# The first layer's weights summed by identity products on TensorE, and one network piece moved ahead of the state products

## The chip, the cores and the metric

The kernel runs on one core of one Trainium2 chip. The metric is the device time of one execution in microseconds (us), lower is better. The engines are named as in the profile: PE is TensorE (PEld its weight loads), DVE is VectorE, ACT is ScalarE, POOL is GpSimd, SP is SyncE, which here only issues transfers.

## The reference

A recurrent attention (batch 4, heads 8, sequence 768, head size 48) is followed by a two-layer network with a PReLU between the layers. The attention's output, laid out as 3072 tokens of 384, is the network's input.

```python
f = sigmoid(f_logit)
for t in range(S):
    state = f[:, :, t, :, None] * state + einsum('bhd,bhe->bhde', k[:, :, t], v[:, :, t])
    y[:, :, t] = einsum('bhd,bhde->bhe', q[:, :, t], state)
x = y.transpose(0, 2, 1, 3).reshape(3072, 384)
h = x @ w_in                                   # 384 x 2048
g = maximum(h, 0) + alpha * minimum(h, 0)
out = g @ w_out                                # 2048 x 384
```

The weights w_in and w_out arrive as 64-bit numbers; the kernel rebuilds them in float32 on the chip.

## The kernel before, in words

**Steps.** The work is cut into 12 steps (lines 725 to 757): 6 chunks of 128 tokens, and in each chunk two pairs of batches. A step handles 2 x 128 = 256 tokens. While step n's attention runs, the network works on step n-1 and the preparation on step n+1.

**Pieces.** Each stage is a Python generator, and each `yield` ends a piece:
- `prepare` (L261; P for the own step, Q for the coming one): loads f, q, k, v; sigmoid and copies on ACT (L282 to L285), then products of decays on DVE (qd L290, kr L293, fs L297), the us copies on ACT (L317), the scans ps and ss (L320, L322), us L324, k L350, the products kh, ks, us, q (L333, L371, L377, L390), and in the last pieces ks L401, us L407, q L409 and the A copies on ACT (L422).
- `carry` (O): first piece the off products (L447, in the first chunk L457 too) with ACT's ad and A copies (L461, L465) and, in the first chunk, the transposes pk (L474) with the ksn copies (L477). Second piece the state products pd (L487) and the update of vs (L497, L501, in the first chunk ACT's copy L503).
- `attend` (S): for each of two batches raw (L523) with the DVE's masked copies (L529) and qu (L538) with its own (L544, in the first chunk L560); then A copies on ACT (L566); then py (L577); then y (L586) on ACT and the transposition to xT, which in step 0 is made on PE (xt L595, ACT copies L597) and later by transfers.
- `network` (n): eight pieces of 6 products ph (L620) with ACT's neg (L625) and two DVE gates (L627), every fourth followed by the sums S (L701); then the second layer, in step 0 plainly (po L640), later with seven half-size products in place of eight (pa to pe, L659).
- `halves_of_w_out` (W, L703): sums of w_out's quarters on DVE (L720) for those seven products.

**The weights.** `load_weights` (L168) makes the pieces of both weights, 8 of 128 x 768 columns each. `upper` (a for w_in, b for w_out) issues a raw transfer on SP (L197; RAWS = 4 buffers) and takes the positive and the negative high parts on ACT, pos (L202) and neg (L204), TOPS = 3 buffers each. `rests` (w for w_in, v for w_out) does lead n (L210, LEADS = 4 buffers), rest n-1 (L223), power n (L216, POWERS = 1) and both n-1, all on DVE but for the last. lead is the high part of a weight in bf16, rest is the low part, put into the weight's place in float32, and `both` adds the high part to it: for w_in's pieces on DVE (L228, since AT_ONCE = 8 takes them all), for w_out's by an accumulating transfer from POOL (L230).

**Order.** PE, DVE and ACT run in exactly the order in which the program issues their instructions (a manual schedule, L745). That order is written by hand: a string for each of the first four steps (`first`, L726 to L731) and one for all others (`usual`, L732). A letter is a piece of the generator with that letter, a number behind it the count of pieces. Transfers are issued by SP and POOL, each in program order.

**PSUM.** Two pools: `pair` has 2 buffers of two banks (off, pk, pd, raw, qu, py), `bank` has 4 buffers of one bank (idle, xt, ph, po, pa to pe). A buffer is given in turn, so an instruction that takes one waits for the readers of the one before.

Of the kernel before, what the change touches and what calls it, by code (L numbers as in the profile page):

```python
# [11 lines left out]
BF16 = mybir.dt.bfloat16  # L12
# [3 lines left out]
ALU = mybir.AluOpType  # L16
# [7 lines left out]
NC2 = C // CH  # L24
NB = DB // 4
WP = 768
AT_ONCE = 8
IDLE = 40
RAWS, TOPS, POWERS, LEADS = 4, 3, 1, 4

# [2 lines left out]
def kernel(  # L33
# [30 lines left out]
    nc = tc.nc  # L64
    B, NC, _, HP, _ = qT.shape
# [7 lines left out]
    W = U * HP * C  # L73
# [15 lines left out]
    const = ctx.enter_context(tc.tile_pool(name="const", bufs=1))  # L89
# [9 lines left out]
    def bank(name):  # L99
        return psn.tile([128, 512], F32, tag="net", name=name)  # L100

    om = const.tile([128, NF], F32, tag="om", name="om")
    w_in_sb = const.tile([128, NK, DF], F32, tag="w_in", name="w_in_sb")
# [31 lines left out]
    for m in range(1, NB):  # L135
        lo = UO[m] + (4 if m == 1 else 0)
        n = NB - m
# [4 lines left out]
    for half in range(2):  # L142
        for m in range(1, NQ):
            n = NQ - m
            lo = 16 * half + 4 if m == 1 else VO[m] + 4 * n * half
# [11 lines left out]
        nc.gpsimd.memset(vs[bp], 0.0)  # L157
    ident = const.tile([128, 128], F32, tag="ident", name="ident")
    make_identity(nc, ident)
    nc.gpsimd.tensor_scalar(om, om, -1.0, 1.0, ALU.mult, ALU.add)  # L160


# [5 lines left out]
    def load_weights(dst, src, name):  # L168

        rows_ = NK if dst is w_in_sb else 1  # L180
        pieces_ = dst.shape[1] * dst.shape[2] // WP
        if rows_ == 1:
            dst = dst.rearrange("p a n -> p (a n)").unsqueeze(1)
        width = WP // rows_
        words = src.rearrange("p (a n) -> p a n", a=rows_).bitcast(I16)
        at_once = AT_ONCE if rows_ > 1 else 0
        got = {}

        def of(n):
            return dst[:, :, n * width:(n + 1) * width]  # L190

        def by_row(t):
            return t.rearrange("p (a n) -> p a n", a=rows_)

        def upper(n):
            raw = stage.tile([128, WP, 4], I16, tag="raw", name=f"{name}_raw{n}", bufs=RAWS)
            nc.sync.dma_start(out=raw.rearrange("p (a n) four -> p a (n four)", a=rows_)[:, :, 0:4 * width - 1],  # L197
                              in_=words[:, :, 4 * n * width + 1:4 * (n + 1) * width])

            top = raw[:, :, 2]  # L200
            pos = stage.tile([128, WP], I16, tag="pos", name=f"{name}_pos{n}", bufs=TOPS)
            nc.scalar.activation(pos, top, AF.Relu, bias=bias[:, 0:1], scale=8.0)  # L202
            neg = stage.tile([128, WP], I16, tag="wneg", name=f"{name}_neg{n}", bufs=TOPS)
            nc.scalar.activation(neg, top.bitcast(U16), AF.Relu, bias=bias[:, 1:2], scale=8.0)  # L204
            got[n] = raw, pos, neg

        def lead(n):
            raw, pos, neg = got[n]
            t = stage.tile([128, WP], BF16, tag="lead", name=f"{name}_lead{n}", bufs=LEADS)
            nc.vector.tensor_tensor(t, pos.bitcast(BF16), neg.bitcast(BF16), ALU.subtract)  # L210
            got[n] = raw, t

        def power(n):
            raw, t = got[n]
            p = stage.tile([128, WP], BF16, tag="power", name=f"{name}_power{n}", bufs=POWERS)
            nc.vector.tensor_scalar(p.bitcast(I16), t.bitcast(I16), -128, None, ALU.bitwise_and)  # L216
            got[n] = raw, t, p

        def rest(n):
            raw, t, p = got.pop(n)  # L220
            got[n] = t
            low = raw.bitcast(U32)[:, :, 0]
            nc.vector.scalar_tensor_tensor(of(n), by_row(low), 2.0 ** -36, by_row(p), ALU.mult, ALU.mult)  # L223

        def both(n):
            t = by_row(got.pop(n))
            if n < at_once:
                nc.vector.tensor_tensor(of(n), of(n), t, ALU.add)  # L228
            else:
                nc.gpsimd.dma_start(out=of(n), in_=t, accum_op=ALU.add)  # L230

        def uppers():
            for n in range(pieces_):
                upper(n)
                yield

        def rests():
            for n in range(pieces_ + 1):
                if n < pieces_:
                    lead(n)  # L240
                if n:
                    rest(n - 1)
                if n < pieces_:
                    power(n)
                if n:
                    both(n - 1)
                yield

        return uppers(), rests()

    def rows(par):
        return slice(64 * par, 64 * par + D)
# [450 lines left out]
    def halves_of_w_out():  # L703
# [12 lines left out]
        for to, x_, y_, op in ((t3, b22, b12, ALU.subtract), (t2, t3, b11, ALU.add), (t4, t2, b21, ALU.subtract),  # L716
                               (b12, b12, b11, ALU.subtract)):
            for h in range(2):
# [5 lines left out]

    steps = [(bp, c) for c in range(NC) for bp in range(B // U)]
    first = (  # L726
# [4 lines left out]
    )  # L731
    usual = "S n2 S n2 O2 n Q n2 Q n2 Q S3 n Q S n Q n Q n"  # L732
    pieces = {key: part for keys, parts in (("aw", load_weights(w_in_sb, w_in, "w_in")),
                                            ("bv", load_weights(w_out_sb, w_out, "w_out")))
              for key, part in zip(keys, parts)}

# [76 lines left out]
```

## Time and profile before

| | |
|---|---|
| median of 3 runs | 633.37 us (632.31 to 634.52) |
| the profiled execution | 634.88 us, of which the span is 633.1 us and 1.8 us lie around it |
| PE busy | 593.9 us, 94% of the span, 8188 instructions |
| PE weight loads busy | 529.2 us, 84% |
| DVE busy | 512.0 us, 81%, 1035 instructions |
| ACT busy | 249.8 us, 39%, 466 instructions |
| POOL busy | 58.8 us, 9%, 107 instructions |
| costliest groups | PE ph L620 258.4 us; PE pa L659 62.0 us and pc L659 61.7 us; DVE gate L627 82.1 us |
| moved by DMA | 53.57 MB; 66% of the 16 engines' time in the first 61.8 us |

How to read it: times are in us from the start of the span, unless marked ns. A timeline line gives start, duration, engine, line of the code, operation, output<-input, the shape and "x" the count of records joined in it; in brackets is the idle time of the engine just before and what released it. A float32 product is two records. A group line ("busy, mean ns of one | idle before, releaser") sums all instructions of one line and form. Matmuls are pipelined, and a few of their records can be missing. "issue" is time in which an engine waited for nothing that the profile shows. The chain of waits is followed back from the last instruction to what released each.

### The profile page before, as it was taken

Reading aid. Unit: us, or ns where it says so; the run is one execution under the profiler, and the core shown is the slowest. Engines: PE = TensorE matmul, PEld = TensorE weight load, DVE = VectorE, ACT = ScalarE, POOL = GpSimd, SP = SyncE. Lnnn points to the kernel's source line nnn. Section 1 sums busy time; section 2 is a strip of 40 time slices with the busy share of each in tenths; the row PEclk is TensorE's granted clock in tenths of the full one; section 3 lists DMA queues with packets and bytes.
Section 4 is the critical chain, followed back from the end, with each engine's and each line's share of the span. In section 5 each row is a group of like instructions: output and inputs, shape, how many; then the busy total and the mean of one; then the engine's idle time right before and its main releaser. Section 6 shows DMA issues by size and latency. Waiting matters only on the chain.

```text
span 633.1 us, 19007 instructions
## 1 busy us (share of the span) xinstructions
PE 593.9 (94%) x8188; PEld 529.2 (84%) x8188; DVE 512.0 (81%) x1035; ACT 249.8 (39%) x466; POOL 58.8 (9%) x107
## 2 busy tenths in 40 slices
PE   2357999989999999999999999999999999999997
PEld 2356865879789889889889889889889889889997
DVE  5799999999799788888888888888888888762251
ACT  5595792541263153253253253253253253223110
POOL 9010122001001001001001001001001000000000
PEclk9999999999999999999999999999999999999999
DMA  7845796312323313313313313323323301201000
GB/s 239 279 146 182 195 295 162 58 62 73 78 54 91 79 35 85 75 46 84 72 48 84 76 45 84 68 52 84 66 54 85 61 26 26 48 7 26 26 0 26
DMA packets 70323, 53.57 MB, mean 85 GB/s; under 512 B 47296, under 2 KB 62144, under 8 KB 70240
## 3 DMA queue, kind: packets, MB, share of 16 engines
q1 hardware_dynamic: 57536, 25.37, 15.9%
q0 software_dynamic: 7312, 24.78, 13.6%
q10 hardware_dynamic: 5392, 2.21, 1.7%
q8 instruction: 65, 1.06, 0.7%
q14 instruction: 18, 0.15, 0.1%
HBM read 36.21 MB, written 4.72 MB: 65 GB/s over the span
## 4 chain that ended last, share of the span: by engine, by line
PE 73%; DVE 22%; issue 2%; ACT 1%; DMA 1%; DVEq 0%; ACTq 0%
PE ph L620 34%; PE pc L659 8%; PE pa L659 8%; PE pe L659 4%; PE pd L659 4%; PE pb L659 4%; PE qu L538 3%; PE py L577 3%; PE raw L523 3%; PE pd L487 2%; DVE gate L627 2%; DVE S L701 2%; DVE us L333 1%; DVE qd L290 1%; DVE ad L529 1%
## 5 line engine op out<-in xcount | busy, mean ns | idle before, releaser
L620 PE MATMUL ph<-xT,w_in_sb 128*128 128x256 f32 x1152 | 258.4, 383 | 0.0
L620 PEld LDWEIGHTS ph<-xT,w_in_sb 128*128 128x128 f32 x1152 | 216.7, 190 | 32.3 <-issue 2.4
L625 ACT ACTIVATE neg<-ph 128x512 f32<-128x512 f32 x96 | 57.2, 596 | 187.4 <-PE ph L620 139.6
L627 DVE SCALAR_TENSOR_TENSOR gate<-neg,om,ph 128x256 f32<-128x256 f32 x192 | 82.1, 474 | 40.7 <-ACT neg L625 40.5
L659 PE MATMUL pa<-w_out_sb,gate 128*128 128x192 f32 x352 | 62.0, 329 | 1.8 <-DVE gate L627 1.8
L659 PE MATMUL pc<-t,S 128*128 128x192 f32 x352 | 61.7, 329 | 0.0
L659 PEld LDWEIGHTS pa<-w_out_sb,gate 128*128 128x128 f32 x352 | 57.8, 190 | 3.7 <-issue 1.9
L659 PEld LDWEIGHTS pc<-t,S 128*128 128x128 f32 x352 | 57.3, 190 | 0.6
L529 DVE COPY_PREDICATED ad<-mraw,raw 128x256 f32<-128x256 int32 (+1 forms) x96 | 42.3, 441 | 7.3 <-PE raw L523 4.8
L544 DVE COPY_PREDICATED ad<-mquad,qu 128x224 f32<-128x224 int32 (+6 forms) x140 | 41.9, 299 | 6.2
L422 ACT COPY A<-q 48x512 f32<-48x512 f32 x44 | 27.2, 617 | 42.4 <-DVE q L371 38.4
L566 ACT COPY A<-ad 32x256 f32<-32x256 f32 x96 | 38.5, 401 | 1.4
L333 DVE TENSOR_TENSOR us<-us,fs 128x768 f32<-128x768 f32 (+5 forms) x60 | 36.7, 612 | 0.1
L677 ACT COPY o<-pa 128x192 f32<-128x192 f32 x11 | 3.5, 318 | 75.3 <-PE pa L659 61.5
L290 DVE TENSOR_TENSOR qd<-qd,f 128x768 f32<-128x768 f32 (+2 forms) x36 | 27.1, 753 | 6.1 <-ACT qd L285 6.1
L538 PE MATMUL qu<-us,k 48*32 48x112 f32 (+1 forms) x1536 | 27.1, 259 | 4.2 <-issue 3.0
L701 DVE TENSOR_TENSOR S<-gate 128x512 f32<-128x512 f32 x44 | 30.3, 688 | 0.8
L659 PE MATMUL pe<-w_out_sb,S 128*128 128x192 f32 x176 | 30.5, 327 | 0.3 <-ACT o L677 0.3
L659 PE MATMUL pb<-t,gate 128*128 128x192 f32 x176 | 30.4, 326 | 0.0
L659 PE MATMUL pd<-w_out_sb,S 128*128 128x192 f32 x176 | 30.4, 326 | 0.0
L577 PEld LDWEIGHTS py<-A,vs 128*64 128x64 f32 x768 | 25.7, 145 | 5.5 <-issue 2.8
L577 PE MATMUL py<-A,vs 128*64 128x64 f32 x768 | 28.1, 233 | 2.0 <-ACT vs L503 1.0
(110 smaller groups left out, 743.0 us busy)
## 6 DMA issues: line engine op xcount, KB each, us to landing
w_out_raw<-in_w_out SPq DMA_DIRECT2D x8, 767.8 KB, 5.0
w_in_raw<-in_w_in SPq DMA_DIRECT2D x8, 767.2 KB, 7.1
f<-in_fT POOLq DMA_DIRECT2D x11, 512.0 KB, 4.5
q<-in_qT POOLq DMA_DIRECT2D x11, 512.0 KB, 4.2
k<-in_kT POOLq DMA_DIRECT2D x11, 512.0 KB, 4.6
out<-o SPq DMA_DIRECT2D x24, 192.0 KB, 2.1
vs<-in_v POOLq DMA_DIRECT2D x22, 192.0 KB, 4.3
w_out_sb<-w_out_lead POOLq DMA_DIRECT2D x8, 384.0 KB, 6.3
```

Of the source, the lines that this page charges most:

```text
L290: nc.vector.tensor_tensor(qdv[d], qdv[d - 1][:, :, :, 1:5 - d], f[:, :, 1:5 - d].rearrange("p (g i) r -> p g i r", i=NB), ALU.mult)
L333: nc.vector.tensor_tensor(us[:, :, UO[m]:UO[m] + 4 * n].rearrange("p g (i r) -> p g i r", r=4), us[:, :, skip:skip + 4 * n].rearrange("p g ...
L529: nc.vector.copy_predicated(adu[:, :, :, d:4], mraw[:, d, :, d:4].bitcast(I32).unsqueeze(1).broadcast_to((128, H, NB, n)), rv[:, :, QO[d]: ...
L538: nc.tensor.matmul(qu[DB * j:DB * (j + 1), par, hp * QS + 4:hp * QS + QL], lhsT=k4[r_, g * DB:(g + 1) * DB], rhs=us[r_, g, 4:QL], start=Tr ...
L544: nc.vector.copy_predicated(ad[:, u, :, :, 4 * m:DB], mquad[:, lo:lo + n].bitcast(I32).unsqueeze(1).unsqueeze(1).broadcast_to((128, 2, HP, ...
L566: nc.scalar.copy(A[s_, u, :, s_], ad[s_, u].rearrange("p r h t -> p (r h) t"))
L577: nc.tensor.matmul(py[64 * par:64 * par + 64, u, o:o + CH], lhsT=vs[bp][:, cc, u, hd * D:hd * D + 64], rhs=A[:, u, par * HP + hp, CH * cc: ...
L620: nc.tensor.matmul(ph[:, j * T:(j + 1) * T], lhsT=w_in_sb[:, kt, m * 128:(m + 1) * 128], rhs=xT[:, kt], start=(kt == 0 and j == 0), stop=( ...
L625: nc.scalar.activation(neg, phv, AF.Relu, scale=-1.0)
L627: nc.vector.scalar_tensor_tensor(gate[:, m % NH, m // NH], neg[:, j], om[:, m:m + 1], phv[:, j], ALU.mult, ALU.add)
L659: nc.tensor.matmul(to[:, 0:DH], lhsT=of(f), rhs=by(f), start=(f == 0 and not more), stop=(f == NH - 1), skip_group_check=True)
L701: nc.vector.tensor_tensor(to, x_, y_, op)
```

## The change

Two things are changed.

1. w_in's high parts are no longer added on DVE. A new generator `sums_of_parts` (key `e`) does for each piece: into a PSUM bank the product of an identity with the float32 low part, and onto it the product of a bf16 identity (`ident16`, a new constant copied on POOL) with the bf16 high part; then ACT copies the bank back to the weight's place. A piece has 3 x 256 columns; the first bank takes 512 of them and a second 256, so a piece is two float32 and two bf16 products and two copies. The banks come from the four of `bank`. w_out's pieces are added by POOL's transfers as before. The four strings of `first` are written anew, with `e` in them: w_in's `a` and `w` come earlier, step 0's network pieces `n` and w_out's `b` and `v` are shifted.

2. In `usual`, "S n2 S n2 O2 n Q n2 Q n2 Q S3" becomes "S n2 S n O n O n Q n3 Q n Q S3"; the rest of the string is as before. On PE one ph piece goes between off (L447) and pd (L487); on DVE the scans (L320, L322) go behind the eighth gate and the sums S.

Lines of the new kernel from `summed` on are 10 higher than before (ph L620 is L630).

```diff
     make_identity(nc, ident)
+    ident16 = const.tile([128, 128], BF16, tag="ident16", name="ident16")
+    nc.gpsimd.tensor_copy(ident16, ident)
...
         def both(n):
+            nc.gpsimd.dma_start(out=of(n), in_=by_row(got.pop(n)), accum_op=ALU.add)
+
+        def summed(n):
             t = by_row(got.pop(n))
-            if n < at_once:
-                nc.vector.tensor_tensor(of(n), of(n), t, ALU.add)
-            else:
-                nc.gpsimd.dma_start(out=of(n), in_=t, accum_op=ALU.add)
+            for lo in range(0, rows_, 2):
+                rs = slice(lo, min(lo + 2, rows_))
+                at = bank(f"{name}_sum{n}_{lo}")[:, 0:width * (rs.stop - lo)].rearrange("p (a n) -> p a n", n=width)
+                nc.tensor.matmul(at, lhsT=ident, rhs=of(n)[:, rs], start=True, stop=False)
+                nc.tensor.matmul(at, lhsT=ident16, rhs=t[:, rs], start=False, stop=True)
+                nc.scalar.copy(of(n)[:, rs], at)
...
-                if n:
+                if n and rows_ == 1:
                     both(n - 1)
                 yield
 
-        return uppers(), rests()
+        def sums_of_parts():
+            for n in range(pieces_):
+                summed(n)
+                yield
+
+        return uppers(), rests(), sums_of_parts()
...
     first = (
-        "P2 a P w P a P a w O P w S a w S Q a S O a w S Q2 w S2",
-        "P a w a P w n b w n v O b v n b S v n2 P S b S v n b S v n b v n Q b n Q v b O v Q n v W Q S2 Q W n2 W Q W",
-        "O n2 S W n2 S Q S n4 O S n Q2 n Q2 S n S n Q n",
-        "S n3 S n Q n2 O Q O n2 S Q S n S Q n Q S Q n3",
+        "P a P a P a w P w P w a P a O a e w2 S2 Q S w e O S e Q2 e S2",
+        "a w n a w P2 n e2 b w n v b O v n b2 S e2 v S3 b v2 n O n b v Q b P v n3 b v Q n S Q v W n S Q n Q W3 Q",
+        "O n S W n2 S n S Q S n4 O Q n Q n S n Q S Q n2 Q",
+        "S n2 S n2 O Q n3 Q n O S n Q S2 Q S n Q n Q n2",
     )
-    usual = "S n2 S n2 O2 n Q n2 Q n2 Q S3 n Q S n Q n Q n"
-    pieces = {key: part for keys, parts in (("aw", load_weights(w_in_sb, w_in, "w_in")),
+    usual = "S n2 S n O n O n Q n3 Q n Q S3 n Q S n Q n Q n"
+    pieces = {key: part for keys, parts in (("awe", load_weights(w_in_sb, w_in, "w_in")),
                                             ("bv", load_weights(w_out_sb, w_out, "w_out")))
               for key, part in zip(keys, parts)}
```

More of the change, by code (lines that the diff above doesn't have):

```diff
@@ L26 @@
 WP = 768
-AT_ONCE = 8
 IDLE = 40
@@ L185, in load_weights @@
         words = src.rearrange("p (a n) -> p a n", a=rows_).bitcast(I16)
-        at_once = AT_ONCE if rows_ > 1 else 0
         got = {}
```

## The prediction

> **What bounds the kernel now.** I read the chain of waits first, then the busy time by stretch, then the timelines of VectorE (DVE), ScalarE (ACT) and TensorE (PE) up to 160 us, and last one usual step. The chain, over the whole span:
>
> ```profile
> PE 73%; DVE 22%; issue 2%; ACT 1%; DMA 1%; DVEq 0%; ACTq 0%
> ```
>
> In order of time it is two stories. Up to 160 us most pieces are DVE, without a break from 89.6 to 160.0 (PE stands in it at 20 to 32 and 62 to 84). After that it is PE. The busy time by stretch (length, then busy us and instructions of PE, PEld, DVE, ACT, POOL, granted clock, DMA share, GB/s) says the same:
>
> ```profile
> 0.00:61.80 61.80, 31.02 (x764) 26.57 (x765) 49.53 (x91) 38.81 (x62) 20.46 (x53) 1.00 0.66 210
> 61.80:160.60 98.80, 95.02 (x1378) 77.53 (x1378) 95.52 (x184) 50.58 (x90) 13.89 (x18) 0.98 0.52 141
> 160.60:633.10 472.50, 467.87 (x6048) 425.14 (x6048) 366.90 (x762) 160.39 (x315) 24.45 (x36) 1.00 0.23 56
> ```
>
> The reader sees: in the first stretch PE is half idle, DMA is two thirds busy and DVE is busy 80%. In the second DVE and PE are both full. In the third PE alone is full, 468 of 472 us. So up to 160 us a DVE us counts, if nothing else is late at the same moment; after that only PE time counts.
>
> The DVE part that is changed, with its neighbours:
>
> ```profile
> 22.86 0.95 DVE L228 TENSOR_TENSOR w_in_sb<-w_in_sb,w_in_lead 128x768 f32<-128x768 f32 x1
> 23.73 0.55 DVE L210 TENSOR_TENSOR w_in_lead<-w_in_pos,w_in_neg 128x768 bf16<-128x768 bf16 x1
> 30.15 1.86 DVE L529 COPY_PREDICATED ad<-mraw,raw 128x256 f32<-128x256 int32 x4 [3.75 <-PE raw L523]
> 33.00 1.01 DVE L560 COPY_PREDICATED ad<-mhalf,qu 128x224 f32<-128x224 int32 x3 [0.99 <-PE qu L538]
> ```
>
> An add takes 0.87 us from its start to the next start. DVE's waits after the start of the kernel are only 3.75, 0.99 and, at 86.99, 0.68 us: 5.4 in all. The DMAs that feed the raw pieces, from the tile's own view:
>
> ```profile
> DMA to landing us min/median/max: 4.9/7.1/14.4
> ```
>
> By piece: raw0 lands at 9.42, raw1 at 17.29, raw3 (14.4 us) at 25.9, raw4 at 29.93 (7.3 us after issue).
>
> **What the Trainium skill says.** "TensorE: Matmul & The Clock Gate", section "What's actually happening": the array runs at half clock by default and after an idle window of about 3.4 us, and at full clock after a window that long of work. The trace agrees in size, though the page's granted-clock row shows no dip: the records of the same matmul form (a float32 product is two records) take 427 ns at 48 us and about 220 ns from 53 us:
>
> ```profile
> 48.10 5.04 PE L595 MATMUL xt<-y,dense 128*128 128x256 f32 x12 [1.72 <-ACT y L586]
> 52.98 5.34 PE L620 MATMUL ph<-xT,w_in_sb 128*128 128x256 f32 x24
> ```
>
> (5.04 / 12 against 5.34 / 24.) "ScalarE: Activation LUTs", section "What ACT_TABLE_LOAD costs": an activation with constants costs 186 ns + 0.833 ns per element, back-to-back ones overlap by 93 ns. For 512 elements that is 613; this trace's PSUM copy of 512 (y, L586) takes 590 with starts 0.53 apart. I use the trace's. "DMA: Bandwidth & Descriptors", section "Issuing engines are not separate DMA queues": all queues interleave on the same 16 engines. The trace agrees: raw3 took 14.4 us while f, q, k and v of the next step were under way.
>
> **The change, part by part.** The base is the profiled execution: 634.88 us, of which the span is 633.1; it stands 1.5 above the median 633.37. A difference found on the span is added to the median.
>
> (1) *DVE adds removed.* 8 x 0.87 = **-6.96 us** of DVE, all before 61.8 us, on the chain.
>
> (2) *PE sums added.* A piece has 768 columns: a float32 product of 512 and one of 256, and the same two in bf16. From the warm ph rate (2 x 0.216 us for 256 columns) float32 is 0.86 + 0.43; a bf16 product isn't in this trace on its own, so I bound it by a half record rate from below (nothing) and one float32 record (0.43 + 0.22) from above, and take 0.33: 1.65 us a piece, 13.2 for 8 warm, about twice that cold. Pieces 0 to 3 fall where PE idles (31 of its first 62 us) and pieces 4 to 7 into 58 to 73 us, 6.6 us of which PE has 2.81 as a wait at 61.82 now (off on DVE us L407). If that cover is gone, the cost is those 6.6 us.
>
> (3) *ACT copies added.* 16 copies, 0.54 + 0.35 a piece, 7.2 us. ACT is busy 38.8 of 61.8 us; none is on the chain by length, only by place in the queue.
>
> (4) *Order of the first steps.* This decides. ACT and PE take their instructions strictly in the written order, so an early piece that waits for its DMA holds up what is behind it. I laid the DVE, ACT and PE queues of the new order end to end, each instruction with its measured duration and its true inputs; the old order laid the same way meets the old trace within 0.5 us up to 160 us. New DVE waits:
> - 1.8 at 13.5, us L324: pos0 and neg0 (0.90 each) now stand ahead of the four us copies L317 on ACT and wait for raw0's landing at 9.42. 9.42 + 1.8 + 4 x 0.54 = 13.4 instead of 11.35.
> - 1.8 at 27.9, lead3: raw3 lands at 25.9, plus pos and neg.
> - 2.6 at 32.2, lead4: LEADS = 4, so it needs piece 0's sum off PE, which stands behind off and pk (end 28.6) and is cold: 3.2 us. Behind this wait on DVE: rest, power, then the raw copies L529, which start at about 33.9 (30.15 before).
> - 1.2 at 38.0: raw1 of the attention, two sums late on PE.
> - 3.6 at 56.1, lead6, and 0.4, lead7: pos6 and neg6 stand on ACT behind the xT copies, which wait for xt, cold, on PE. So they did before, but DVE came to lead6 at 57.8 and found neg6 done at 55.3; now it comes at 52.5. Behind lead6 on DVE stand rest, power and the q, ks and us products of the coming step, which off (L447, L457) waits for:
>
> ```profile
> 53.18 0.37 ACT L597 COPY xT<-xt 128x256 f32<-128x256 f32 x1 [0.92 <-PE xt L595]
> 53.45 1.01 ACT L202 ACTIVATE w_in_pos<-w_in_raw,bias 128x768 int16<-128x768 int16 x1
> 54.34 1.01 ACT L204 ACTIVATE w_in_neg<-w_in_raw,bias 128x768 int16<-128x768 uint16 x1
> ```
>
> - 0.9 (gate 3), 1.2, 1.9, 0.7 (w_out lead2, 4, 5: pos and neg later on ACT, or the DMA accumulate still reading), 0.3 (qd): 5.0 from 72 to 92 us.
>
> Together 16.4 us. The old order laid in the same way has 6.5, measured 5.4: **+10 to +11**. Net at the last w_out rest (101.1 before): -7 + 10 to 11 = +3 to +4.1. PE cross-check: off L447 at 109.83, plus 6.6 of sums, less the 2.81 wait, less some 1 us of cold time that the sums take over = +2.8. Both agree. DVE and PE are both full from there to 160 us, so it is passed on whole; no slack absorbs it later, as PE has 4.6 us not busy in 472.
>
> (5) *POOL and SP queues.* One more copy on POOL (ident16, 128x128) before the loads start; f of the next step ahead of its vs loads, the w_out accumulates and out stores keep their order. SP's raw DMAs wait on rests (51.1 us by SP's waits), which move by the amounts above. I take 0, from -1 to +1 (raw4 and raw5 in or out of the crowd).
>
> (6) *Usual steps.* One ph group of 3 x 2 products (L620) is put between off (L447) and pd (L487); the scans L320 and L322 go behind the eighth gate and S. The same work. Can off wait? It needs its PSUM pair free, so the raw copies L529 done:
>
> ```profile
> 312.51 5.45 PE L620 MATMUL ph<-xT,w_in_sb 128*128 128x256 f32 x24
> 317.88 0.76 PE L447 MATMUL off<-q,kh 48*32 48x32 f32 x64
> 318.71 1.65 PE L487 MATMUL pd<-vs,ksn 64*48 64x48 f32 x64
> 312.26 1.87 DVE L529 COPY_PREDICATED ad<-mraw,raw 128x256 f32<-128x256 int32 x4
> ```
>
> (The last line is from DVE's timeline.) The copies end at 314.1; off would start at 315.2. 1.1 us of margin, so 0. There is at most a 0.07 us gap between off and pd, and PE's idle in a step is about 0.5 us, so bounds are -0.3 and +0.1 a step over 9 steps: -2.7 to +1.
>
> Sum: -7 + 10.6 + 0 + 0 = **+3.6: 637.0 us**. The unknowns around it (raw4 landing 9 instead of 7.2 us after issue, clock gate phase +-1.3, w_out DMAs faster -2.4, slower ACT copies) give it 635.3 to 640.
>
> **The rivals.**
> - *No change, 633.4 us (chance 0.17).* The waits come out 3.5 smaller than laid, so they equal the 7 us saved, or the usual edit pays 0.3 x 9 = 2.7. For: the DVE waits at 72 to 92 us (5.0) hang on DMA latencies of the new order, which no row shows. Against: lead3, lead4 and lead6 rest on landings that the trace shows.
> - *Faster, about 629 (0.13).* The halves are ready when DVE asks: lead3, lead4 and lead6 (1.8 + 2.6 + 3.6 = 8.0) don't wait, so 3.6 - 8.0 = -4.4. It decides at ACT's neg6: done before DVE finishes the vs adds (about 52.5 us) it costs nothing. For: raw DMAs are asked for earlier in the new order. Against: neg6 stands behind xT, and xt needs y, which needs py.
> - *A larger loss, about 641 (0.12).* raw4 lands 2 us later than I take, in DMA at its fullest, or the sums run cold also at 58 to 73 us (another 6.6, partly hidden). +4 on top.
> - That the change doesn't do what it says: the adds are off DVE by the code, so no case.
>
> Main case 0.58. **The numbers.** About 0.3%, 1.9 us, is what a measurement of this kernel can tell from no change. Main and larger loss are slower: 0.70; same 0.17; faster 0.13. The range of 632.5 to 642.0 leaves out the faster case and a little at the top.
>
> **What would show it.** DVE's timeline without L228 and with idle before lead4, lead6 and us L324 of about 2.6, 3.6 and 1.8 us; ACT's us copies ending at about 13.4; raw copies L529 first at about 34; off of step 2 at about 112.7; usual steps 47.9 us apart as before. Wrong if lead3, lead4 and lead6 show no idle time, or if a usual step differs by more than 0.1 us.

## The result, and the profile after

The changed kernel took 632.31 us (median of 22 runs, 629.65 to 636.27), the kernel before in the same comparison 633.35 us (22 runs): a ratio of 0.9982, 95% interval 0.9971 to 0.9992. It is 1.0 us faster, not 3.6 slower. The two profiled executions lie apart by more than that, 634.88 (before) and 630.05 (after); the first is 1.5 above its median and the second 2.3 below. A stage-by-stage comparison of these two alone would therefore find 3.8 us that no median shows. I compare stages over all the profiles made in this study.

The chain of waits after, over the span, and the busy time in the same stretches as before (PE, PEld, DVE, ACT and POOL, then granted clock, DMA share and GB/s). In the chain PE fell from 73% to 56% and ACT rose from 1% to 11%, while the time hardly moved. This suggests that several engines are late by nearly the same; the chain names only the last.

```profile
PE 56%; DVE 21%; ACT 11%; issue 7%; DMA 3%; POOL 1%; SPq 0%; ACTq 0%; DVEq 0%; POOLq 0%
```
```profile
0.00:61.80 61.80, 37.91 (x744) 29.15 (x748) 46.64 (x89) 43.60 (x74) 19.68 (x54) 0.97 0.71 230
61.80:160.60 98.80, 95.19 (x1458) 76.75 (x1465) 91.44 (x173) 49.42 (x90) 13.87 (x18) 1.00 0.48 129
160.60:628.30 467.70, 462.64 (x6049) 420.32 (x6032) 367.49 (x767) 161.02 (x318) 24.36 (x36) 1.00 0.24 57
```

Up to 160 us DVE's busy time fell from 145.1 to 138.1 us: the 7 us of adds are gone. But the work of 160 us did not get 7 us shorter. Off of step 2, the first product that the third step makes on PE, started at 109.83 before and at 110.00 after. The 7 us became waits. DVE's timeline of the changed kernel has these (I count all from 8 us to off of step 2; the lines are the five longest):

```profile
13.27 1.23 DVE L334 TENSOR_TENSOR us<-us,f 128x1024 f32<-128x1024 f32 x1 [1.44 <-ACT us L327]
30.59 0.56 DVE L210 TENSOR_TENSOR w_in_lead<-w_in_pos,w_in_neg 128x768 bf16<-128x768 bf16 x1 [2.85 <-ACT A L475]
53.36 0.56 DVE L210 TENSOR_TENSOR w_in_lead<-w_in_pos,w_in_neg 128x768 bf16<-128x768 bf16 x1 [1.66 <-ACT w_in_neg L204]
74.49 0.56 DVE L210 TENSOR_TENSOR w_out_lead<-w_out_pos,w_out_neg 128x768 bf16<-128x768 bf16 x1 [2.42 <-DMA w_out_sb<-w_out_lead]
82.82 0.56 DVE L210 TENSOR_TENSOR w_out_lead<-w_out_pos,w_out_neg 128x768 bf16<-128x768 bf16 x1 [1.91 <-ACT w_out_neg L204]
```

With 1.33, 0.34, 0.22 and 0.20 they make 12.4 us; before they were 5.4. At 30.59 the profile names ACT's A copies as the releaser; they were issued for something else. What lead4 waits for is the first sum on PE, whose last product was at 30.20 (a second profile of the same kernel names it: "PE w_in_sum L234", 3.84 us).

From 160 us on the span is 4.8 us shorter (467.7 instead of 472.5). A usual step, from off of step 4 to off of step 11 over 7, takes 47.35 us instead of 47.86. PE's timeline shows where:

```profile
310.85 2.86 PE L630 MATMUL ph<-xT,w_in_sb 128*128 128x256 f32 x12
313.64 0.76 PE L457 MATMUL off<-q,kh 48*32 48x32 f32 x64
314.32 2.86 PE L630 MATMUL ph<-xT,w_in_sb 128*128 128x256 f32 x12
317.11 0.94 PE L497 MATMUL pd<-vs,ksn 64*48 64x48 f32 x64
317.98 10.63 PE L630 MATMUL ph<-xT,w_in_sb 128*128 128x256 f32 x48
```

The same 32 products pd (64 records) take 0.94 us behind ph, where they took 1.65 behind off. No idle time stood in front of them before: the 0.7 us were inside the row's duration. Off and pd together went from 2.40 us (317.88 to 320.28) to 0.68 + 0.87. py, on the other hand, went from a mean of 2.08 to 2.39 (also from its start to the next start; the rows' own durations are some 0.07 longer).

### The profile page after: what moved, and what is told of

Read it like the earlier page. It is cut to its first block, busy times and chain, and to the rows that moved or that the text cites. A ratio compares the mean times of both kernels' runs of the same rounds, so it can differ in the third digit from the quotient of the medians.

```text
span 628.3 us, 19113 instructions
## 1 busy us (share of the span) xinstructions
PE 595.7 (95%) x8231; PEld 526.2 (84%) x8236; DVE 505.6 (80%) x1027; ACT 254.1 (40%) x482; POOL 57.9 (9%) x108
## 4 chain that ended last, share of the span: by engine, by line
PE 56%; DVE 21%; ACT 11%; issue 7%; DMA 3%; POOL 1%; SPq 0%; ACTq 0%; DVEq 0%; POOLq 0%
PE ph L630 20%; PE pc L669 9%; PE pa L669 6%; PE pe L669 5%; PE pd L669 5%; DVE gate L637 4%; ACT A L576 4%; DVE S L711 3%; DVE qd L300 3%; PE qu L548 3%; ACT us L327 3%; PE raw L533 3%; DMA w_in_raw<-in_w_in 2%; PE py L587 2%; PE pb L669 2%
## 5 line engine op out<-in xcount | busy, mean ns | idle before, releaser
L630 PE MATMUL ph<-xT,w_in_sb 128*128 128x256 f32 x1152 | 260.0, 383 | 0.4 <-DVE Csum L691 0.4
L630 PEld LDWEIGHTS ph<-xT,w_in_sb 128*128 128x128 f32 x1152 | 215.4, 190 | 32.6 <-issue 2.4
L669 PEld LDWEIGHTS pd<-w_out_sb,S 128*128 128x128 f32 x176 | 28.9, 190 | 0.0
L669 PEld LDWEIGHTS pe<-w_out_sb,S 128*128 128x128 f32 x176 | 28.9, 190 | 0.0
L669 PEld LDWEIGHTS pb<-t,gate 128*128 128x128 f32 x176 | 28.9, 190 | 0.0
L587 PEld LDWEIGHTS py<-A,vs 128*64 128x64 f32 x768 | 24.1, 138 | 5.5 <-issue 3.1
```

Source lines behind the costliest of these rows:

```text
L587: nc.tensor.matmul(py[64 * par:64 * par + 64, u, o:o + CH], lhsT=vs[bp][:, cc, u, hd * D:hd * D + 64], rhs=A[:, u, par * HP + hp, CH * cc: ...
L630: nc.tensor.matmul(ph[:, j * T:(j + 1) * T], lhsT=w_in_sb[:, kt, m * 128:(m + 1) * 128], rhs=xT[:, kt], start=(kt == 0 and j == 0), stop=( ...
L669: nc.tensor.matmul(to[:, 0:DH], lhsT=of(f), rhs=by(f), start=(f == 0 and not more), stop=(f == NH - 1), skip_group_check=True)
```

## The experiments

"Before" in each line is the kernel before on the same chip. Each timed kernel had 4 to 22 runs.

**1. The usual string alone.**

```diff
-    usual = "S n2 S n2 O2 n Q n2 Q n2 Q S3 n Q S n Q n Q n"
+    usual = "S n2 S n O n O n Q n3 Q n Q S3 n Q S n Q n Q n"
```

> The kernel before with only the usual string of the change. Theory A (the usual edit is what pays: pd right behind ph takes 0.94 us instead of 1.65 right behind off, and py gives back 0.3): a step is 47.35 us instead of 47.86, 9 x -0.5 = -4.6, so about 628.8 us, with pd at 0.9. Rival, my recorded step (6) (the edit is worth 0, -2.7 to +1): 630.7 to 634.4, likeliest 633.4.

Measured: 629.51 us, ratio 0.9944 (0.9932 to 0.9956), 3.5 us less. A step took 47.37 us, pd 0.94. Theory A stands: 8 steps, not 9, have an off and a pd (the last loop has only the network left), and 8 x 0.49 is 3.9. My step (6) falls.

**2. The sums and the four new strings, old usual string.**

> The changed kernel with the usual string of before: sums on TensorE and the four new strings alone. Theory A (my recorded +3.6 for the first steps holds, and the usual edit paid 4.6): about 637.0 us. Rival B (in the profiled executions the first steps differ by only +0.3 up to step 3, so the sums and strings cost nothing): 633.4 to 633.7 us. Rival C (the small total is all there is, the usual edit pays nothing): 632.3 us.

Measured: 635.18 us, ratio 1.0040 (1.0024 to 1.0055), 2.3 to 2.5 us more. +2.4 and -3.5 give -1.1: the parts add up to the result. The edit whose cost I had worked out lost time, as forecast in sign; the edit that I put at nothing gained more.

**3. What pd's 0.7 us are.** From the step on in which ksn comes by 16 transfers, whose semaphores pd has to see, nine separate wait instructions stand on PE's queue: three ahead of pd's first product and two ahead of each of the next three. "Perfetto Trace Analysis", section "Identifying Dependency Chains", of the Trainium skill says that an instruction waiting for several engines may have wait instructions inserted ahead of it. The trace of before shows what they cost. In the step above, the nine lie between 318.39 and 319.36, each 0.05 us long; there is a gap of 0.15 to 0.23 us and then one product (2 weight loads, 2 records), four times over, and then no more gaps of that kind. To separate this from the sheer number of short instructions, I kept off and pd neighbours and took the waits earlier, on one tiny product in front of off. Its result goes to an unused corner.

```diff
         off = pair(f"off_{i}")
+        if c:
+            nc.tensor.matmul(off[0:4, 1, 500:502], lhsT=x["ksn"][:, 0, 0:128:32], rhs=vs[bp][:, :, 0, 0], start=True, stop=True)
```

> The kernel before, with one tiny product (ksn and vs, 4 columns by 2) in front of the off products, into a corner of off's PSUM that nobody reads, so that TensorE takes its waits for ksn's transfers there, behind ph, and no longer in front of pd. off and pd stay neighbours. Theory A (pd's 0.7 us are the nine wait instructions between its first products, which nothing hides behind the short off products): pd falls from 1.65 to about 0.9 us and a step from 47.86 to about 47.2, so about 627 us. Rival (256 short instructions in a row outrun the supply of instructions): pd stays at 1.65 us and the time at 633.4 or slightly more.

Measured: 644.78 us, ratio 1.0186 (1.0173 to 1.0200): slower, and for the most part by one stall, which is in PE's timeline of this run, in the first step whose ksn comes by transfers:

```profile
121.16 0.19 PE L441 MATMUL off<-vs,ksn 128*4 128x2 f32 x2 [13.69 <-DMA ksn<-kt]
```

There ksn had not landed, and off and all behind it stood behind the wait. My expectation had overlooked that step. The usual steps answer the question asked, though:

```profile
329.69 0.19 PE L441 MATMUL off<-vs,ksn 128*4 128x2 f32 x2
329.81 0.76 PE L449 MATMUL off<-q,kh 48*32 48x32 f32 x64
330.50 0.94 PE L489 MATMUL pd<-vs,ksn 64*48 64x48 f32 x64
331.37 10.63 PE L622 MATMUL ph<-xT,w_in_sb 128*128 128x256 f32 x48
```

pd right behind off takes 0.94 us. So neither the neighbour nor the count of short instructions makes it slow, but the wait instructions in its midst. Behind ph they are hidden: in the changed kernel's step shown above, the nine lie between 314.24 and 316.05, while the ph piece between off and pd still runs.

**4. The same from step 4 on** (`if c > 1:` in place of `if c:`).

> The kernel before with the tiny product in front of off as in the earlier run, but only from step 4 on, where the usual string is used and ksn has long landed. Theory A (wait instructions are the 0.7 us, and the loss of the earlier run was its one stall of 14.3 us where ksn had not landed): off plus pd 1.55 us and 0.15 for the probe instead of 2.4, a step 0.6 shorter, 8 steps: about 628 us. Rival (the tiny product costs as much as it saves): 633.

Measured: 628.42 us, ratio 0.9921 (0.9904 to 0.9937), 5.0 less. A step took 47.25 us, 0.61 less, and 8 of them 4.9. Theory A holds, and no ph piece was moved for it. Off of step 2 came at 107.19; in experiment 3, with the product in steps 2 and 3 too, at 121.28.

**5. py's 0.3 us: A copies ahead of kept.**

```diff
-    usual = "S n2 S n O n O n Q n3 Q n Q S3 n Q S n Q n Q n"
+    usual = "S n2 S n O n O n Q n3 Q S n Q S2 n Q S n Q n Q n"
```

> The kernel before with the usual string of the change, in which the first A copies piece (S) stands ahead of the second layer's first piece (n) on ScalarE and no longer behind it. Theory A (py's 0.3 us a step are a new wait for A copies, made by the 0.85 us that pd gives): py goes back from 2.37 to about 2.1 us, a step from 47.37 to about 47.1, so about 2 us below the new usual string alone (629.5): 627.3. Rival (py is slower for another reason, or something else takes the place): 629.5.

Measured: 630.39 us, ratio 0.9955 (0.9940 to 0.9971); py took 2.46 us. A miss: the wait was for A copies, but not because of kept (L667). ACT's timeline of experiment 1 shows what does stand ahead:

```profile
329.20 0.60 ACT L625 ACTIVATE neg<-ph 128x512 f32<-128x512 f32 x1 [2.35 <-DVE gate L627]
329.69 2.19 ACT L317 COPY us<-qd 128x256 f32<-128x256 f32 x4
331.62 0.42 ACT L667 COPY Csum<-pa 128x192 f32<-128x192 f32 x1
331.89 3.33 ACT L566 COPY A<-ad 32x256 f32<-32x256 f32 x8
```

The new string puts three network pieces behind the qd products on DVE (n3), so the eighth neg waits 2.35 us for a gate, and the us copies and A copies queue behind it.

**6. A copies in that gap.**

```diff
-    usual = "S n2 S n O n O n Q n3 Q n Q S3 n Q S n Q n Q n"
+    usual = "S n2 S n O n O n Q n2 S n Q n Q S2 n Q S n Q n Q n"
```

> The kernel before with the usual string of the change, the first A copies piece (S) put in front of the eighth network piece, where ScalarE waits 2.4 us for VectorE's gates. In the run with A copies ahead of kept, they came after the us copies and py still waited. Theory A (py waits for A copies because the us copies stand before them): py 2.08 instead of 2.38, a step about 47.07 us instead of 47.37, 8 steps: 627.1 us against 629.5 for the new usual string alone. Rival (something else takes the place, as ScalarE's neg of the eighth ph comes later): 629.5.

Measured: 625.73 us, ratio 0.9884 (0.9869 to 0.9899), 7.3 to 7.9 less than before. py 2.02, a step 47.00. In ACT's timeline of this run the copies fill what was idle, at no cost to the neg behind them:

```profile
323.55 1.64 ACT L566 COPY A<-ad 32x256 f32<-32x256 f32 x4
326.00 0.60 ACT L625 ACTIVATE neg<-ph 128x512 f32<-128x512 f32 x1 [0.82 <-DVE gate L627]
```

**7. The sums behind each w in the old strings.**

> The kernel before with w_in's adds replaced by the sums on TensorE and ScalarE, each put directly behind its w piece in the strings of before, usual string of before. Theory A (the order of the new strings, not the sums, brings the waits that eat the 7 us): the adds go from VectorE, but each sum stands on TensorE and ScalarE where the step's own products wait, so about 630 to 634 us, and in any case less than the new strings with the old usual. Rival (the sums themselves cost it): 637 or more.

Measured: 667.71 us, ratio 1.0555 (1.0540 to 1.0569). A large miss of mine. PE takes its instructions in order, and a sum directly behind its w waits for VectorE's rest with everything behind it; from the waits of this run (us in total, times, longest):

```profile
PE w_in_sum L233 <- DVE w_in_sb L223: 43.6, 7, 16.2
```

So the sums can't stand directly behind their w; other places for them in the old strings were not tried.

**8. The new order with the adds on VectorE.** `summed` does the add of before (L228), at the places of `e`.

```diff
-                nc.tensor.matmul(at, lhsT=ident, rhs=of(n)[:, rs], start=True, stop=False)
-                nc.tensor.matmul(at, lhsT=ident16, rhs=t[:, rs], start=False, stop=True)
-                nc.scalar.copy(of(n)[:, rs], at)
+            nc.vector.tensor_tensor(of(n), of(n), t, ALU.add)
```

> The changed kernel, in which the e pieces are VectorE adds again (one e is put ahead of its neighbour w, since a buffer ring asks for it), at the places of the new strings; no sums on TensorE or ScalarE. Theory A (in the new order VectorE's waits, 12 us, and not its work decide; the adds fall into them): 631 to 635 us, near the changed kernel. Rival (each add counts on VectorE as in the kernel before): 7 us more than the changed kernel, 639 us.

Measured: 635.44 us, ratio 1.0030 (1.0015 to 1.0045), against 631.63 for the changed kernel in the same comparison: 3.8 more. Between the theories. Off of step 2 came at 117.06, 6.1 to 7.1 later than in two profiles of the changed kernel: in this profile each add counts up to there. By off of step 4 (223.88 against 218.91 and 220.05) some 2 us are given back.

**9. The changed kernel again.**

> The changed kernel again, as a control on the same chip and for a second profile of its first 110 us. Theory A: about 632.3 us; off of step 2 at 110.0 in the first profile, here later if this execution is a slower one, with longer waits of VectorE for raw pieces or w_out. Rival: the first 110 us are the same in every execution, and the spread of 629.7 to 636.3 us comes from later.

Measured: 631.63 us, ratio 0.9980 (0.9968 to 0.9991), and a second profile: off of step 2 at 110.94, DVE's waits up to there 13.2 us instead of 12.4. The first 110 us do vary from execution to execution, and with the waits.

**10. The sums left out in the new order** (`summed` only drops its piece; w_in lacks its high parts).

> The changed kernel without the sums: the e pieces do nothing, so w_in lacks its high parts; 16 us of TensorE and 7 us of ScalarE are left out and nothing takes their place. Theory A (the sums lie in TensorE's and ScalarE's idle time up to 61.8 us and cost only what they add to the full TensorE from 56 to 72 us, 6.6 us partly hidden): 628 to 630 us. Rival (the sums are free, the waits of the new order are all there is): 632 us. Rival (the sums stand in everything's way): 625 us or less.

Measured: 632.49 us, ratio 0.9977 (0.9964 to 0.9989): the same as with the sums. So the sums, 16 us of PE and 7 of ACT, cost nothing on balance. Their price alone this run does not give, as the array was slower without them in the profiled execution. From 58 to 75 us the granted clock was 0.80 of full speed here and 1.00 in both profiles of the changed kernel, and off of step 2 came later, at 114.12 (this execution was 2 us above its median). Here are the xt products of this run, and then those of the changed kernel:

```profile
47.16 4.86 PE L599 MATMUL xt<-y,dense 128*128 128x256 f32 x12 [1.17 <-ACT y L590]
```
```profile
48.29 2.86 PE L605 MATMUL xt<-y,dense 128*128 128x256 f32 x12 [2.23 <-ACT y L596]
```

**11. The adds left out in the old order** (w_in lacks its high parts here too; 7 us of VectorE are left out and nothing takes their place).

> The kernel before without w_in's adds on VectorE and nothing in their place, so w_in lacks its high parts; order of before. Recorded step (1) (each VectorE us before 61.8 counts): 7 us less, 626.3. Rival (TensorE is full from 61.8 us and waits for landings of the raw pieces stand beside, so a part comes back as waits): 629 to 631 us.

Measured: 632.29 us, ratio 0.9985 (0.9968 to 1.0002), 0 to 2 us less. This is the run that hits step (1). DVE's waits of this run up to off of step 2, the two longest of seven, 10.8 us in all:

```profile
29.40 1.87 DVE L527 COPY_PREDICATED ad<-mraw,raw 128x256 f32<-128x256 int32 x4 [4.90 <-PE raw L521]
66.48 0.56 DVE L210 TENSOR_TENSOR w_out_lead<-w_out_pos,w_out_neg 128x768 bf16<-128x768 bf16 x1 [1.53 <-ACT w_out_neg L204]
```

Off of step 2 came at 109.64, as before. PE's raw and ACT's pos and neg were next to late, and took over what the adds gave up.

**12. us copies first in the changed kernel** ("P2 a2 P a w" for "P a P a P a w").

> The changed kernel with the first pieces of its first string in the order P2 a2 P a w instead of P a P a P a w, so that ScalarE makes the us copies before it waits for the first raw piece. Theory A (the 1.4 us that VectorE waits at us L334 pass on to off and to all after it): off of step 0 at 18.6 instead of 20.0 and about 1.4 us less, 630.5. Rival (a landing or the first sum sets the later wait at lead4, so the 1.4 us come back there): no change, 632.

Measured: 632.46 us, ratio 0.9989 (0.9977 to 1.0001). The wait of 1.4 us at 13.3 is gone, off of step 0 is at 18.85, and nothing is won, as lead4 waits longer (4.64 instead of 2.85 and 3.84):

```profile
31.23 0.56 DVE L210 TENSOR_TENSOR w_in_lead<-w_in_pos,w_in_neg 128x768 bf16<-128x768 bf16 x1 [4.64 <-ACT A L475]
```

The rival was right: the first sum sets that point, from whichever side DVE comes to it. The sum in turn stands behind off and pk, and in the midst of off PE stands still with "issue", for nothing that the profile shows. Here are the kernel before, the changed kernel and this run; in a second profile of the changed kernel it is 1.82 us, up to 26.17:

```profile
26.12 0.71 PE L457 MATMUL off<-us 48*32 48x16 f32 x49 [4.83 <-issue]
```
```profile
25.63 0.71 PE L467 MATMUL off<-us 48*32 48x16 f32 x49 [1.27 <-issue]
```
```profile
25.96 0.71 PE L467 MATMUL off<-us 48*32 48x16 f32 x49 [2.77 <-issue]
```

PE came to this place some 1.2 us earlier than in the changed kernel, and went on at about the same time.

**13. The repaired usual string behind three sets of first strings**, on one chip.

> The changed kernel with the usual string that has the A copies piece in ScalarE's gap. Theory A (the usual string's gain is independent of the first strings): py from 2.39 to about 2.05 us a step, 8 steps, 2.8 us less than the changed kernel: 629 us, which stays about 2 above the same usual string behind the old strings. Rival (the new strings cost nothing and the gain adds up): 626 us.

> The kernel before with the new strings of steps 2 and 3 and the usual string with the A copies piece in the gap; strings of steps 0 and 1 and the adds as before. Theory A (the cost is in steps 0 and 1 alone; from off of step 2 to off of step 4 the new strings are 0.8 us shorter in the profiles): 625 us or a little less than the old strings. Rival (the strings of steps 2 and 3 bring the cost): 627 to 628 us.

> Control: the kernel before with only the usual string that has the A copies piece in the gap, again. Theory A: 625.7 us as in the first run, a step of 47.0 us. Rival (part of the 7.9 us was that chip or that build): 627 us, which is what 8 steps of 0.86 us give.

Measured, against before: all new strings 629.36 us, 0.9916 (0.9899 to 0.9932); new strings of steps 2 and 3 only 625.70, 0.9863 (0.9850 to 0.9877); none 626.92, 0.9885 (0.9871 to 0.9899). The repair carries over to the changed kernel: 0.9916 against its 0.9982 and 0.9980 is about 4 us, and a step takes 46.99 us instead of 47.35, which is 2.9 for eight. The new strings with the sums still lose 2.4 us behind it. The strings of steps 2 and 3 alone gain 1.2 (the two intervals overlap a little), so the loss should lie in steps 0 and 1; their new strings were not run alone. The mixed version, with the old strings in steps 0 and 1, the new ones in steps 2 and 3 and no sums, is the best of the study, 8.4 us less than the kernel before.

## Why the prediction was wrong, step by step

**One account for the first 110 us.** Over the profiles of fourteen executions (all but those of experiments 3, 7 and 8), the start of off of step 2, less DVE's waits between 8 us and there, plus 7.0 us where the adds are not on DVE, is 104.2 to 106.0 us. Old strings with adds, seven profiles: waits 2.7 to 6.1, mean 4.3. New strings with sums, five profiles: 12.4 to 14.8, mean 13.1. So -7.0 + 13.1 - 4.3 = +1.9, and the timed kernels say +2.4. The mechanism of the likeliest case is confirmed: waits took the place of the adds. (The kernel with the adds in the new order stands a little outside, at 106.5.)

**Step (6), usual steps: this failed.** "The same work ... so 0", with bounds of -2.7 to +1, and it was -3.5. That is most of the 4.6 us between forecast and result; the rest lies in the first steps, mostly in step (4). The sign that I had named for being wrong, a usual step that differs by more than 0.1 us, came. I asked whether off could start, and looked for idle time between off and pd. The time was inside pd's own row. The page before had shown it, had I held the 1.65 us against the other pd in the same trace, which stands behind po (in step 1, where ksn comes by copies on ACT and pd has none of these wait instructions):

```profile
89.57 0.94 PE L487 MATMUL pd<-vs,ksn 64*48 64x48 f32 x64
```

The same number of products, 0.7 us shorter. By -0.7 (pd), -0.13 (off), -0.15 (pa, whose gate is no longer behind the scans), +0.2 (ph, in one more piece) and +0.3 (py) a step comes to -0.5.

**Step (1), -6.96: right in size, wrong as a gain.** DVE's busy time fell by it. But experiment 11 shows that this order yields 0 to 2 us for it. I put all eight adds "before 61.8 us, on the chain". Two of them start later, at 64.36 and 67.11, and the chain of before has only four:

```profile
35.74 0.87 DVE w_in_sb L228
44.81 0.87 DVE w_in_sb L228
51.68 0.87 DVE w_in_sb L228
59.52 0.95 DVE w_in_sb L228
```

At the other four, the two late ones and those at 22.86 and 25.45, the chain stands on PE. So 3.6 us was the most that the chain promised, and even of these it says who was last, not by how much.

**Step (2), sums: right.** 1.65 us a piece against 1.61 measured warm (two pieces from 56.17 to 59.40) and 2.4 to 3.5 for the first two, cold; 16 us in all. What they cost the kernel in all is nothing that could be measured (experiment 10), less than I feared. (0.86 + 0.43 + 0.33 is 1.62 and not 1.65, and the 16 copies of step (3) come to 7.1 and not 7.2; neither matters.)

**Step (4), waits: sized too large, mainly for two reasons.** 16.4 laid, 12.4 to 14.8 measured. lead3 waited not at all, as raw3 landed at about 21.1 and not at 25.9: I had taken a landing of the old order for the new one; its pos stood ready before DVE asked. lead6 waited 1.66, not 3.6: I had priced xt cold, as in the trace before (5.04 us), and behind the sums the array was warm (2.86). lead4 (2.6; 2.85 to 4.8), us L324 (1.8; 1.4) and w_out lead4 (1.9; 1.9) were as laid. w_out lead2 was longer (1.2; 2.3 to 2.5), and us L334 of step 1 (1.3 to 1.5 at 46 to 49 us, behind the sums' copies on ACT) I had not.

**The rivals.** The result lies in the case "no change" (0.17). It gave as one way that the usual edit pays, 0.3 us a step; it paid 0.5. With 0.5 put in place of 0, and everything else kept, the forecast would have been 633.1. The faster rival, halves that are ready, did not happen: lead4 and lead6 waited in all profiles of the changed kernel, and of the three only lead3 did not.

**What stays open.** By experiment 13 the new strings are dearer in steps 0 and 1, and the sums on balance are not the cause; experiment 12 took away one of their waits and it came back at the next. Which order of these two steps would let the adds' 7 us be won was not tried. One stall stands in every one of the fourteen profiles, and neither the prediction nor the account names it: behind 79 of the 128 records of the same group of off, in step 0, PE stands still for 1.3 to 5.1 us and goes on at 24.8 to 26.7. In the kernel before it makes up 4.83 of the 12 us for which the chain stands on PE there. A 16 KB packet on the queue that the page calls "instruction" starts 2.5 to 3.0 us ahead of its end each time. So PE may have waited for its own instructions there; no experiment tests it.

## What to carry to other kernels

Compare an instruction group's duration with that of the same group in another neighbourhood of the same trace: time that is lost in it shows as no wait. A group with many semaphores to see (here of 16 transfers) was 0.7 us dearer behind short instructions than behind long ones. An earlier, well hidden instruction can take the waits, once its data have surely landed.

Work taken off an engine that is on the chain is worth only the distance to what is next to late; here 0 to 2 of 7 us. A kernel that leaves the work out altogether gives that bound before anything is built in its place.

## What was not expected of the hardware

Nine wait instructions cost about 0.7 us on PE when nothing long was ahead of them, and nothing that shows behind ph.

More work went with a faster PE. The sums lie in front of xt: in all six profiles with the sums xt's 12 records took 2.86 us, in ten of the eleven without them 4.3 to 5.5. The eleventh (experiment 8) took 2.86 too, so it can happen without the sums. This is the half clock of "TensorE: Matmul & The Clock Gate" in "What's actually happening", which the page of the Trainium skill puts down to idle windows. The trace's clock records agree where there are any: before, they give 0.50 from 62.8 to 66.2 us, just behind PE's wait of 2.8 us that ends at 61.82. But they begin only at 52.6 us there, as xt ends. So the 1.00 that the prediction read for the first stretch says nothing of xt.
